# Chunk attention and two expert layers: the value products of one tile and the scores of the next put into one sequence

## The chip, the cores and the metric

The kernel runs on one core of a Trainium2 chip. The metric is the device time of one execution in microseconds (us). Six engines are named: PE (TensorE, matmuls), PEld (its weight loads), DVE (VectorE), ACT (ScalarE), POOL (GpSimd) and SP (SyncE, which issues DMAs).

## The reference

Three stages follow one another; the output of each is the input of the next.

```python
# 1. attention inside chunks of 64: q, k, v of (8 batches, 8 heads, 576, 64)
scores = (q_c @ k_c^T) / sqrt(64);  scores -= max(scores)
attn = exp(scores);  attn = attn / (sum(attn) + 1e-9);  x = attn @ v_c
x -> (4608 tokens, 512)
# 2. first layer: d_model 512, d_ff 1536
g = x @ w_gate;  x2 = (g * sigmoid(g) * (x @ w_val)) @ w_out
# 3. second layer: d_ff 2048
h = x2 @ w_in;  out = (h - tanh(h)) @ w_out2
```

## The kernel before

**Layers.** Tokens are worked in 9 blocks of 512. The hidden columns of a layer are worked in pairs of 128-wide tiles. The first layer makes two sweeps over the blocks with three pairs each (sweep 0 and sweep 1), the second layer one sweep with eight pairs. One pair of one block is a *unit* of 22 slots. Numbers are split into a high and a low part and multiplied in three passes, so a product of two blocks is a group of matmuls "x3" or "x6". The in-projections use a scheme of seven block products (inputs named B11, B21, T2, T1, T3, B22, T4, tiles `xb_*`); their outputs are `Xg, Yg` (gate) and `Xv, Yv` (value), in banks m0 and m1. DVE and ACT make the two parts of each `xb` tile: a cast (the high part, steps `x0.hB11` and so on) and a subtraction (the low part, `x0.lB11`). The out-projections are `acc`, in banks o0 to o3. In the page L1239 is the out-projection and L660 an in-projection.

**Attention.** It runs inside sweep 0, one block ahead: during the three units of block t-1 the four tiles of block t are worked, each a pair of heads (tile numbers 8 to 35, function `heads`) or a group of tokens (4 to 7, `tokens`; 0 to 3 run at the start and are called early). Steps of a tile, with their names in the tables: q and k are loaded (`lq`, SP) and turned (`tq`, `tk`, DVE), v is loaded (`lv`, POOL's queue). PE makes 16 products of 64x64 for each half of the tile, `sc` (step `s`, L887, 32 matmuls in all). DVE takes the maximum and subtracts it (`c0`, `c1`: tiles `mx`, `scratch`), ACT takes the exponential (`e`), DVE the sums (`n`, tile `sm`) and the division (`m`, L302), PE turns the result (`p`, `ppt`, L823), ACT copies it, PE makes the products with v, `po` (step `o`, L898, 32 matmuls), and ACT copies these to the block's x, `xra`. Both `sc` and `po` lie in PSUM banks a0 and a1, a pair of tiles each, one after the other; `ppt` too lies in a0.

**Order.** Nothing is scheduled on the chip: a table `AT` gives each step a slot relative to the start of its set (`START`, for attention tiles a0 to a3 in each block), `ON` names the engine (A for ACT, V for DVE), and `tick` issues, after each piece of PE work, all steps whose slot has come. Every engine then works its instructions in that order. A PE piece is one group of six in-projection matmuls or three out-projection matmuls.

Of the kernel before, what the change touches and what calls it, by code (L numbers as in the profile page):

```python
# [10 lines left out]
F32 = mybir.dt.float32  # L11
# [18 lines left out]
    "ah.ld": -6.5, "ah.mag": 9.5, "ah.cl": 11.5, "ah.sh": 11.5, "ah.sg": 12.5, "ah.tl": 13,  # L30
# [12 lines left out]
    "g1.l0": 19.5, "g1.h1": 22, "g1.l1": 23, "a.lq": -19.5, "a.lv": 4, "a.tq": -8.5, "a.tk": -4,  # L43
    "a.s": 0, "a.c0": 1.5, "a.c1": 2.5, "a.e": 3, "a.n": 7, "a.m": 9, "a.p": 12.5, "a.o": 14.5,
    "ge.silu0": 14.5, "ge.silu1": 12.5, "ge.m1": 21, "ge.m0": 20.5, "ge.h0": 23, "ge.l0": 24.5,
    "ge.h1": 24, "ge.l1": 32, "dr.ld": -19.5, "dr.mag": 9, "dr.cl": 11, "dr.sh": 11.5,
    "dr.sg": 13, "dr.tl": 13, "dr.h": 16.5, "dr.l": 17.5, "dc.ld0": -14, "dc.mag0": 0,
# [195 lines left out]
def chunk_attention_moe_moe(  # L243
# [14 lines left out]
    nc = tc.nc  # L258
# [5 lines left out]
    HP = H // 2  # L264
    C = 64
# [1212 lines left out]
```

## Time and profile before

| | |
|---|---|
| median of 3 runs | 1757.7 us (1754.9 to 1758.71) |
| profiled execution | 1756.21 us, its span 1754.4 us |
| mean granted clock of TensorE | 0.994 of full speed |
| PE busy | 1712.4 us (98%) |
| DVE busy | 1381.9 us (79%) |
| ACT busy | 1135.8 us (65%) |

The span falls into four parts here: the start (0 to 100 us, attention of the first block, weights are split), the rest of sweep 0 (100 to 500 us, with the attention of the later blocks in it), the passage to sweep 1 (500 to 600 us), and the rest. A row of the windows view gives, for a stretch "from:to", its length, then the busy time and the number of instructions of PE, PEld, DVE, ACT and POOL, then TensorE's granted clock, the share of the DMA engines and GB/s. A row of the timeline gives the start of a group of like instructions, the time from its first start to its last end, engine, line, operation and tile; in brackets the idle time before it and what ended it. Neighbouring PE groups overlap in that view, because matmuls are pipelined: what a group costs is read from start to start. A row of the waits view gives what waited, for what, the time in total, how often, and the longest.

### The profile page before, as it was taken

What the parts mean: (1) busy time and instruction counts of PE and PEld (TensorE: products, weight loads), DVE (VectorE), ACT (ScalarE), POOL (GpSimd) and SP (SyncE); (2) the same over time, 40 slices, a digit from 0 to 9 for tenths busy, and PEclk for the clock granted to TensorE, in tenths of its full rate; (3) what the DMA queues carried; (4) which work ended last, traced back from release to release, by engine and by line L of the source; (5) the groups of instructions that cost most, each with busy time, mean ns of one, the idle gap of its engine ahead of it and who ended that gap; (6) DMA issues with size and microseconds to landing.
All of it is one profiled execution on the core that took longest, in us unless ns stands there. A gap on an engine that the chain in (4) does not pass through costs nothing.

```text
span 1754.4 us, 33741 instructions
## 1 busy us (share of the span) xinstructions
PE 1712.4 (98%) x12880; PEld 1531.7 (87%) x12880; DVE 1381.9 (79%) x2613; ACT 1135.8 (65%) x2209; POOL 136.5 (8%) x238
## 2 busy tenths in 40 slices
PE   5999999999999999999999999999999999999999
PEld 4778888888898999999999898899999898998997
DVE  6998778887878987787875678787877878787876
ACT  4765565566555655545554578787777777777776
POOL 2133333322100000000000000000000000000000
PEclk8999999999999999999999999999999999999999
DMA  9554554555423555555545744343434343434333
GB/s 244 143 109 115 142 134 123 128 145 138 131 101 120 193 186 169 180 186 186 169 167 191 260 174 145 107 145 97 151 102 144 105 148 97 149 104 144 99 130 109
DMA packets 238482, 254.94 MB, mean 145 GB/s; under 512 B 150000, under 2 KB 175472, under 8 KB 236016
## 3 DMA queue, kind: packets, MB, share of 16 engines
q1 hardware_dynamic: 230896, 243.33, 45.4%
q0 software_dynamic: 7424, 9.45, 2.1%
q8 instruction: 101, 1.65, 0.4%
q14 instruction: 61, 0.50, 0.1%
HBM read 187.17 MB, written 65.54 MB: 144 GB/s over the span
## 4 chain that ended last, share of the span: by engine, by line
PE 83%; DVE 8%; SPq 4%; DMA 3%; ACT 1%; issue 1%; DVEq 0%; ACTq 0%
PE acc L1239 36%; PE Xi L660 12%; PE Yi L660 9%; PE Xg L660 6%; PE Xv L660 6%; PE Yv L660 5%; PE Yg L660 5%; SPq L849 3%; DMA raw_wv<-in_moe_w_val_dram 1%; SPq L947 1%; DMA kr<-in_k_dram 1%; DVE scratch L299 1%; PE po L898 1%; PE sc L887 1%; PE ppt L823 1%
## 5 line engine op out<-in xcount | busy, mean ns | idle before, releaser
L1239 PE MATMUL acc<-wp,h 128*128 128x512 f32 x1728 | 479.9, 394 | 0.0
L1239 PE MATMUL acc<-h,wo 128*128 128x512 f32 x1296 | 364.1, 397 | 0.0
L1239 PEld LDWEIGHTS acc<-wp,h 128*128 128x128 f32 x1728 | 290.9, 188 | 33.4 <-DVE h L299 0.3
L1239 PEld LDWEIGHTS acc<-h,wo 128*128 128x128 f32 x1296 | 220.4, 189 | 28.6
L338 ACT CAST h<-gs 128x512 fp32r<-128x512 f32 x144 | 89.5, 621 | 86.0 <-DVE gs L1150 84.5
L864 POOL DMA_DIRECT2D vr<-in_v_dram x200 | 116.2, 599 | 283.9 <-PE po L898 259.9
L660 PEld LDWEIGHTS Xg<-xb_T,wg 128*128 128x128 f32 x864 | 122.2, 188 | 13.0
L660 PE MATMUL Xg<-xb_T,wg 128*128 128x256 f32 x864 | 125.9, 281 | 0.0
L296 DVE TENSOR_TENSOR gs<-Yi,s 128x256 f32<-128x256 f32 x144 | 60.8, 422 | 64.9 <-PE Yi L660 59.5
L1073 ACT ACTIVATE gs<-gs 128x512 f32<-128x512 f32 x96 | 60.8, 633 | 58.0 <-DVE gs L296 57.8
L299 DVE TENSOR_TENSOR vr<-gs,vr 128x512 f32<-128x512 f32 x72 | 49.9, 692 | 54.6 <-ACT vr L1126 54.6
L299 DVE TENSOR_TENSOR h<-gs,h 128x512 fp32r<-128x512 f32 x144 | 92.7, 684 | 0.2 <-ACT h L338 0.2
L338 ACT CAST h<-vs 128x512 fp32r<-128x512 f32 x107 | 66.3, 622 | 37.1 <-PE acc L1239 25.2
L299 DVE TENSOR_TENSOR h<-vs,h 128x512 fp32r<-128x512 f32 x108 | 73.6, 682 | 20.3 <-ACT h L338 19.5
L660 PE MATMUL Yv<-xb_B,wv 128*128 128x256 f32 x576 | 85.4, 283 | 2.0 <-ACT s L338 1.9
L660 PE MATMUL Xv<-xb_T,wv 128*128 128x256 f32 x576 | 86.2, 285 | 0.8 <-ACT sqr L338 0.8
L660 PE MATMUL Yg<-xb_B,wg 128*128 128x256 f32 x576 | 84.2, 281 | 0.0
L660 PEld LDWEIGHTS Yg<-xb_B,wg 128*128 128x128 f32 x576 | 78.8, 189 | 5.1
L660 PEld LDWEIGHTS Yv<-xb_B,wv 128*128 128x128 f32 x576 | 75.4, 188 | 6.1 <-ACT s L338 4.6
L660 PEld LDWEIGHTS Xv<-xb_T,wv 128*128 128x128 f32 x576 | 75.1, 189 | 1.4 <-ACT sqr L338 1.0
L338 ACT COPY s<-Xi 128x256 f32<-128x256 f32 x144 | 53.5, 372 | 34.9 <-PE Xi L660 30.9
L302 DVE TENSOR_TENSOR vs<-vs,gs 128x512 f32<-128x512 f32 x96 | 65.8, 686 | 8.1 <-ACT gs L1073 5.3
(310 smaller groups left out, 3732.7 us busy)
## 6 DMA issues: line engine op xcount, KB each, us to landing
wp<-split_wp SPq DMA_DIRECT2D x144, 512.0 KB, 3.5
split_wi<-wi SPq DMA_DIRECT2D x24, 512.0 KB, 3.4
xd<-xra SPq DMA_DIRECT2D x36, 256.0 KB, 3.1
x2p<-ob SPq DMA_DIRECT2D x36, 256.0 KB, 2.6
xr_xd<-xd SPq DMA_DIRECT2D x9, 1024.0 KB, 4.8
ob<-x2p SPq DMA_DIRECT2D x36, 256.0 KB, 4.2
x2d<-ob SPq DMA_DIRECT2D x36, 256.0 KB, 2.4
xr_x2d<-x2d SPq DMA_DIRECT2D x9, 1024.0 KB, 6.0
```

Of the source, the lines that this page charges most:

```text
L296: eng.tensor_tensor(out=out_, in0=a, in1=b, op=ALU.add)
L299: eng.tensor_tensor(out=out_, in0=a, in1=b, op=ALU.subtract)
L302: eng.tensor_tensor(out=out_, in0=a, in1=b, op=ALU.mult)
L338: eng.copy(out_, in_)
L660: nc.tensor.matmul(bank, w[:, wl, kk * 128:(kk + 1) * 128], x[xn][:, xl, kk, :], start=start and n == 0, stop=n == 5, skip_group_check=not ...
L823: nc.tensor.transpose(pt[:, m, :], z["p"][:, m].rearrange("p e j -> p (e j)"), ident)
L849: nc.sync.dma_start(out=r[p:p + 32, 2 * n:2 * (n + m)], in_=src[b, 2 * j + e, s:s + m * C, d * 32:d * 32 + 32] .rearrange("(n p) d -> p n ...
L864: nc.gpsimd.dma_start(out=vr[p:p + C, n + skip:n + m:2], in_=chunks[:, skip:m:2],)
L887: nc.tensor.matmul(sc[e ^ c][c * C:(c + 1) * C, m, :], z["qT"][h, cut], z["kT"][h, cut], start=True, stop=True,)
L898: nc.tensor.matmul(po[c][h, m, :], z["vr"][f, 2 * m + c, :], z["pT"][f, m, c * C:(c + 1) * C], start=True, stop=True,)
L1073: return lambda: nc.scalar.activation(out=gs[i], in_=gs[i], func=AF.Silu)
L1239: nc.tensor.matmul(u["acc"][d], l, r, start=p0 and i == 0 and n == 0, stop=p1 and i == 1 and n == 2,)
```

## The change

Two functions made the `sc` and the `po` of a tile by themselves. Now a function `burst(g, n)` makes the `po` of tile g and the `sc` of tile n = g+1 in one sequence, four of the one and four of the other in turn, into a pair of tiles in banks a0 and a1 that hold both: `po` in the first half of a bank, `sc` in the second. It stands at the step `o` of tile g. Step `s` is gone for tiles 5 to 35; tile 4's scores come alone (`burst(None, 4)`) and tile 35's products with v alone. The early tiles 0 to 3 stay as they were. So there were 64 sequences of 32 matmuls outside the early tiles, and there are now 31 of 64 matmuls and two of 32.

```diff
+    def burst(g, n):
+        bank = [
+            ps.tile([128, 2, 4, C], F32, tag=f"a{c}", name=f"po{g}_sc{n}_{c}") for c in range(2)
+        ]
+        half = [slice(0, C), slice(C, 2 * C)]
+        if g is not None:
+            z = att[g]
+            z["po"] = [bank[c][:, 0] for c in range(2)]
+        if n is not None:
+            y = att[n]
+            y["sc"] = [bank[e][:, 1] for e in range(2)]
+            done.add((("a", n), "s"))
+        for m in range(4):
+            if g is not None:
+                for c in range(2):
+                    for e in range(2):
+                        f = half[e ^ c]
+                        nc.tensor.matmul(
+                            z["po"][c][half[e], m, :], z["v_"](f, m, c), z["pT"][f, m, half[c]],
+                            start=True, stop=True,
+                        )
+            if n is not None:
+                for c in range(2):
+                    for e in range(2):
+                        nc.tensor.matmul(
+                            y["sc"][e ^ c][half[c], m, :],
+                            y["q_"](half[e], m, c), y["k_"](half[e], m, c),
+                            start=True, stop=True,
+                        )
...
         def output(eng):
-            po = [ps.tile([128, 4, C], F32, tag=f"a{c}", name=f"po{g}_{c}") for c in range(2)]
...
+            burst(g, g + 1 if g + 1 < NG else None)
+            po = z["po"]
...
-        step("s", scores, ["tq", "tk"])
```

Beside it the tables for sweep 0 have other numbers: 267 of the 614 slots that both tables name. Of attention's steps `c0`, `c1` and `e` keep their slots after a tile's start; the rest are later or earlier:

```diff
-    "g1.l0": 19.5, "g1.h1": 22, "g1.l1": 23, "a.lq": -19.5, "a.lv": 4, "a.tq": -8.5, "a.tk": -4,
-    "a.s": 0, "a.c0": 1.5, "a.c1": 2.5, "a.e": 3, "a.n": 7, "a.m": 9, "a.p": 12.5, "a.o": 14.5,
+    "g0.l1": 33.5, "g1.silu0": 16, "g1.silu1": 21, "g1.m1": 22, "g1.m0": 16.5, "g1.h0": 18.5,
+    "g1.l0": 23, "g1.h1": 23, "g1.l1": 27, "a.lq": -23.5, "a.lv": 8, "a.tq": -3, "a.tk": -3,
+    "a.c0": 1.5, "a.c1": 2.5, "a.e": 3, "a.n": 8, "a.m": 9.5, "a.p": 13.5, "a.o": 16.5,
...
-    "units": 60, "a0": -12, "a1": 4, "a2": 20, "a3": 38, "ah0": 140, "ah0 every": 22,
+    "units": 60, "a0": -12, "a1": 4.5, "a2": 21, "a3": 38, "ah0": 140, "ah0 every": 22,
```

Fifteen entries of `ON` differ. Five casts of the next block (`x0.hB11`, `x0.hB21`, `x0.hT2`, `x0.hT3`, `x0.hB22`) go from DVE to ACT, two of sweep 1 (`x1.hT3`, `x1.hT4`) from ACT to DVE, and eight single steps change sides.

**PE, around the products with v of tile 24.** The rows of before, where a block of six or three matmuls is one row:

```order
L823 MATMUL ppt24_4607<-ident_81,scratch0_175 128x128 x4
L660 MATMUL Xg0_5_0_4631<-xb14_B11_4497,wg0_0_592 128x256 x6
L660 MATMUL Yg0_5_0_4632<-xb14_B21_4499,wg0_0_592 128x256 x6
L898 MATMUL po24_0_4654<-scratch0_175,vr24_4532 64x64 x2
...
L898 MATMUL po24_1_4655<-scratch0_175,vr24_4532 64x64 x2
L1239 MATMUL acc0_4_0_0_4357<-h0_4_1_1_4381,wo1_1_1252 128x512 x3
L660 MATMUL Xg0_5_0_4631<-xb14_T2_4515,wg0_1_1656 128x256 x6
L887 MATMUL sc0_25_4688<-kT25_4605,qT25_4570 64x64
L887 MATMUL sc1_25_4689<-kT25_4605,qT25_4570 64x64 x2
```

And the same place after the change:

```order
L822 MATMUL ppt24_4590<-ident_81,scratch0_175 128x128 x4
L659 MATMUL Yg0_5_0_4581<-xb14_B21_4472,wg0_0_590 128x256 x6
L1260 MATMUL acc0_4_0_0_4300<-h0_4_1_1_4392,wo1_1_1255 128x512 x3
L659 MATMUL Xg0_5_0_4580<-xb14_T2_4475,wg0_1_1660 128x256 x6
L850 MATMUL po24_sc25_0_4624<-scratch0_175,vr24_4524 64x64 x2
L850 MATMUL po24_sc25_1_4625<-scratch0_175,vr24_4524 64x64 x2
L857 MATMUL po24_sc25_0_4624<-kT25_4598,qT25_4596 64x64
L857 MATMUL po24_sc25_1_4625<-kT25_4598,qT25_4596 64x64 x2
L857 MATMUL po24_sc25_0_4624<-kT25_4598,qT25_4596 64x64
L850 MATMUL po24_sc25_0_4624<-scratch0_175,vr24_4524 64x64 x2
```

The scores of tile 25 stood two pieces behind the products with v; now both are one run of rows that write the same two tiles. Three pieces instead of two stand between `ppt24` and the products.

**DVE, from the maximum of tile 24 to its division, in the third unit of a block.** Before; the names in brackets are the engines that the row waits for:

```order
L796 TENSOR_REDUCE mx24_0_4493<-sc0_24_4465 128x4 [waits PE_49]
...
L340 CAST xb14_B11_4497<-xra5_3825 128x512 [waits PE_49]
L340 CAST xb14_B21_4499<-xra5_3825 128x512 [waits PE_49]
...
L340 CAST xb14_T2_4515<-scratch1_2011 128x512 [waits PE_49]
...
L873 STREAM_TRANSPOSE qT25_4570<-qr25_4401 128x512 [waits DMAHW4_49,DMAHW5_49,DMAHW3_49,DMAHW6_49,DMAHW2_49,DMAHW7_49,DMAHW1_49,DMAHW0_49]
L296 TENSOR_TENSOR vs0_4_2_0_4509<-Yv0_4_2_4484,s0_4_2_4485 128x256 [waits PE_49]
L340 CAST xb14_T3_4580<-xra5_3825 128x512 [waits DVE_49]
L302 TENSOR_TENSOR scratch0_175<-scratch0_175,sm24_4565 128x512
```

After:

```order
L795 TENSOR_REDUCE mx24_0_4455<-po23_sc24_0_4407 128x4 [waits Activation_49]
...
L298 TENSOR_TENSOR xb14_B21_4472<-xra5_3819,xb14_B21_4472 128x512 [waits Activation_49]
...
L301 TENSOR_TENSOR scratch0_175<-scratch0_175,sm24_4533 128x512 [waits DVE_49]
L298 TENSOR_TENSOR xb14_T1_4508<-xra5_3819,xb14_T1_4508 128x512 [waits Activation_49]
L298 TENSOR_TENSOR xb14_T3_4510<-xra5_3819,xb14_T3_4510 128x512 [waits Activation_49]
L301 TENSOR_TENSOR vs0_4_2_0_4465<-vs0_4_2_0_4465,gs0_4_2_0_4298 128x512
L907 STREAM_TRANSPOSE qT25_4596<-qr25_4328 128x512 [waits DMAHW4_49,DMAHW5_49,DMAHW3_49,DMAHW6_49,DMAHW2_49,DMAHW7_49,DMAHW1_49,DMAHW0_49]
L907 STREAM_TRANSPOSE kT25_4598<-kr25_4337 128x512 [waits DMAHW4_49,DMAHW5_49,DMAHW3_49,DMAHW6_49,DMAHW2_49,DMAHW7_49,DMAHW1_49,DMAHW0_49]
```

The first maximum waited for PE; now it waits for ACT, whose two copies of `po23` (out of the same banks) come first. Between it and the division 21 rows stood, now 15: the four casts are on ACT, and the turn of q of tile 25 (and one addition to `h`) stand outside this stretch.

## Rows read from the trace of the kernel before

**Rows 1.** Page, busy time of each engine and share of the span.

```profile
PE 1712.4 (98%) x12880; PEld 1531.7 (87%) x12880; DVE 1381.9 (79%) x2613; ACT 1135.8 (65%) x2209; POOL 136.5 (8%) x238
```

**Rows 2.** Windows view, four parts of the span: length, PE, PEld, DVE, ACT, POOL.

```profile
0.00:100.00 100.00, 77.01 (x812) 59.96 (x813) 80.71 (x178) 59.94 (x106) 24.82 (x46) 0.90 0.79 185
100.00:500.00 400.00, 390.43 (x4007) 339.87 (x4006) 323.71 (x685) 240.16 (x453) 111.67 (x192) 1.00 0.52 128
500.00:600.00 100.00, 95.64 (x652) 87.41 (x652) 83.51 (x173) 58.55 (x128) 0.00 (x0) 1.00 0.44 155
600.00:1754.40 1154.40, 1149.36 (x7415) 1044.43 (x7413) 893.98 (x1581) 777.14 (x1524) 0.00 (x0) 1.00 0.44 147
```

**Rows 3.** Waits view of PE, 100 to 500 us: total, times, longest.

```profile
PE ppt L823 <- DVE scratch L302: 6.5, 8, 1.1
PE Yv L660 <- ACT s L338: 1.3, 5, 0.4
PE po L898 <- ACT scratch L338: 0.9, 4, 0.2
```

**Rows 4.** Timeline of PE around one sequence of scores: start, duration, group.

```profile
308.32 0.88 PE L660 MATMUL Xv<-xb_T,wv 128*128 128x256 f32 x6
309.12 0.69 PE L887 MATMUL sc<-kT,qT 64*64 64x64 f32 x32
309.75 0.96 PE L1239 MATMUL acc<-h,wo 128*128 128x512 f32 x3
310.54 0.52 PE L660 MATMUL Yv<-xb_B,wv 128*128 128x256 f32 x3
```

**Rows 5.** The same view where no 64x64 sequence stands between.

```profile
314.08 0.87 PE L660 MATMUL Yg<-xb_B,wg 128*128 128x256 f32 x6
314.79 0.86 PE L1239 MATMUL acc<-h,wo 128*128 128x512 f32 x3
315.49 0.87 PE L660 MATMUL Xg<-xb_T,wg 128*128 128x256 f32 x6
```

**Rows 6.** One line's matmuls, L898: shortest, median and longest in ns, first and last start.

```profile
L898 PE MATMUL po<-scratch,vr x896: 218/218/268, 110.9 to 494.2; 64*64 64x64 f32 x180
```

**Rows 7.** Timeline of PE in the start, two 64x64 sequences on end.

```profile
31.57 0.96 PE L998 MATMUL sc<-kT,qT 64*64 64x64 f32 x32
32.35 1.11 PE L1025 MATMUL po<-pp,vr 64*64 64x64 f32 x32
33.39 0.66 PE L823 MATMUL ppt<-ident,pp 128*128 128x128 f32 x4
```

**Rows 8.** Windows view, a third unit of a block and a stretch in that start.

```profile
330.40:349.80 19.40, 18.18 (x177) 15.85 (x175) 17.49 (x38) 11.58 (x22) 4.51 (x8) 1.00 0.45 116
...
32.30:33.40 1.10, 1.10 (x49) 1.03 (x41) 1.10 (x3) 0.00 (x0) 0.00 (x0) 1.00 1.19 278
```

**Rows 9.** Timeline of DVE, from the maximum of tile 24 to its division.

```profile
323.60 0.42 DVE L796 TENSOR_REDUCE mx<-sc 128x4 f32<-128x256 f32 x1 [0.70 <-PE sc L887]
...
325.00 0.78 DVE L340 CAST xb_B<-xra 128x512 fp32r<-128x512 f32 x2
...
327.42 0.42 DVE L340 CAST xb_T<-scratch 128x512 fp32r<-128x512 f32 x1
...
332.08 0.70 DVE L873 STREAM_TRANSPOSE qT<-qr 128x512 f32<-128x512 f32 x1
...
333.34 0.68 DVE L302 TENSOR_TENSOR scratch<-scratch,sm 128x512 f32<-128x512 f32 x1
```

**Rows 10.** Timeline of PE, the transposition that waits for that division.

```profile
334.17 0.63 PE L823 MATMUL ppt<-ident,scratch 128*128 128x128 f32 x4 [1.07 <-DVE scratch L302]
```

**Rows 11.** Timeline of ACT behind the products with v of tile 24.

```profile
337.44 0.65 ACT L338 COPY xra<-po 128x256 f32<-128x256 f32 x2 [0.95 <-PE po L898]
...
341.50 1.28 ACT L801 ACT_TABLE_LOAD   x1
```

**Rows 12.** Waits view of PE, 500 to 600 us, the two largest.

```profile
PE Yg L660 <- DVE gs L296: 1.7, 1, 1.7
PE Xg L660 <- DVE vs L296: 1.1, 1, 1.1
```

More of the change, by code (lines that the diff above doesn't have):

```diff
@@ L29 @@
 AT = {
-    "ah.ld": -6.5, "ah.mag": 9.5, "ah.cl": 11.5, "ah.sh": 11.5, "ah.sg": 12.5, "ah.tl": 13,
[12 rows of a table removed]
-    "g1.l0": 19.5, "g1.h1": 22, "g1.l1": 23, "a.lq": -19.5, "a.lv": 4, "a.tq": -8.5, "a.tk": -4,
-    "a.s": 0, "a.c0": 1.5, "a.c1": 2.5, "a.e": 3, "a.n": 7, "a.m": 9, "a.p": 12.5, "a.o": 14.5,
-    "ge.silu0": 14.5, "ge.silu1": 12.5, "ge.m1": 21, "ge.m0": 20.5, "ge.h0": 23, "ge.l0": 24.5,
-    "ge.h1": 24, "ge.l1": 32, "dr.ld": -19.5, "dr.mag": 9, "dr.cl": 11, "dr.sh": 11.5,
-    "dr.sg": 13, "dr.tl": 13, "dr.h": 16.5, "dr.l": 17.5, "dc.ld0": -14, "dc.mag0": 0,
[3 rows of a table removed]
+    "ah.ld": -13, "ah.mag": 10.5, "ah.cl": 12, "ah.sh": 13, "ah.sg": 13.5, "ah.tl": 28.5,
[12 rows of a table added]
+    "g1.l0": 23, "g1.h1": 23, "g1.l1": 27, "a.lq": -23.5, "a.lv": 8, "a.tq": -3, "a.tk": -3,
+    "a.c0": 1.5, "a.c1": 2.5, "a.e": 3, "a.n": 8, "a.m": 9.5, "a.p": 13.5, "a.o": 16.5,
+    "ge.silu0": 20, "ge.silu1": 20, "ge.m1": 24, "ge.m0": 21.5, "ge.h0": 23.5, "ge.l0": 24,
+    "ge.h1": 29, "ge.l1": 34.5, "dr.ld": -22.5, "dr.mag": 9, "dr.cl": 11, "dr.sh": 11.5,
+    "dr.sg": 13, "dr.tl": 13, "dr.h": 16.5, "dr.l": 17.5, "dc.ld0": -13.5, "dc.mag0": 0.5,
[3 rows of a table added]
     "dc.l1": 24, "dc.h2": 22, "dc.l2": 26, "fc2.ld0": -2, "fc2.ld1": 11, "fc2.ld2": -4,
@@ L827, in turn_p @@
         return f
+    att = {}
+    def burst(g, n):
[7 more added lines that the diff above has]
+        if n is not None:
+            assert (("a", n), "tq") in done and (("a", n), "tk") in done
+            y = att[n]
[18 more added lines that the diff above has]
+                        )
     def heads(g, start):
@@ L876, in turn, with chunk @@
             return f
-        def scores():
-            sc = z["sc"] = [
-                ps.tile([128, 4, C], F32, tag=f"a{e}", name=f"sc{e}_{g}") for e in range(2)
-            ]
-            for m in range(4):
-                for c in range(2):
-                    cut = slice((2 * m + c) * C, (2 * m + c + 1) * C)
-                    for e in range(2):
-                        h = slice(e * C, (e + 1) * C)
-                        nc.tensor.matmul(
-                            sc[e ^ c][c * C:(c + 1) * C, m, :], z["qT"][h, cut], z["kT"][h, cut],
-                            start=True, stop=True,
-                        )
-        def output(eng):
-            po = [ps.tile([128, 4, C], F32, tag=f"a{c}", name=f"po{g}_{c}") for c in range(2)]
-            for m in range(4):
-                for c in range(2):
-                    for e in range(2):
-                        h, f = slice(e * C, (e + 1) * C), slice((e ^ c) * C, ((e ^ c) + 1) * C)
-                        nc.tensor.matmul(
-                            po[c][h, m, :], z["vr"][f, 2 * m + c, :],
-                            z["pT"][f, m, c * C:(c + 1) * C],
-                            start=True, stop=True,
-                        )
+        def chunk(nm):
+            return lambda h, m, c: z[nm][h, (2 * m + c) * C:(2 * m + c + 1) * C]
+        att[g] = z
+        z["q_"], z["k_"] = chunk("qT"), chunk("kT")
+        z["v_"] = lambda f, m, c: z["vr"][f, 2 * m + c, :]
+        def output(eng):
+            burst(g, g + 1 if g + 1 < NG else None)
+            po = z["po"]
             if j == 0:
@@ L934, in tokens @@
         else:
-            banks = dict(q="a0", k="a1", s=("a0", "a1"), p="a0", o="a1")
+            banks = dict(q="a0", k="a1", p="a0")
+            att[g] = z
+            z["q_"] = lambda h, m, c: z["qT"][h, m, c * C:(c + 1) * C]
+            z["k_"] = lambda h, m, c: z["kT"][h, m, c * C:(c + 1) * C]
+            z["v_"] = lambda f, m, c: z["vr"][f, c, m, :]
         def load_qk():
@@ L998, in scores @@
                         nc.tensor.matmul(
-                            sc[e if early else e ^ c][i, hp, :], z["qT"][h, hp, i], z["kT"][h, hp, i],
+                            sc[e][i, hp, :], z["qT"][h, hp, i], z["kT"][h, hp, i],
                             start=True, stop=True,
@@ L1013, in output @@
                 po = ps.tile([128, HP, 128], F32, tag=banks["o"], name=f"po{g}")
-                whole, po = po, [po[:, :, :C], po[:, :, C:]]
-            else:
-                po = [
-                    ps.tile([128, HP, C], F32, tag=banks["s"][c], name=f"po{g}_{c}")
-                    for c in range(2)
-                ]
-            for hp in range(HP):
-                for c in range(2):
-                    for e in range(2):
-                        h, i = slice(e * C, (e + 1) * C), slice(c * C, (c + 1) * C)
-                        f = h if early or c == 0 else slice((1 - e) * C, (2 - e) * C)
-                        nc.tensor.matmul(
-                            po[c][h, hp, :], z["vr"][f, c, hp, :], z["pT"][f, hp, i],
-                            start=True, stop=True,
-                        )
+                for hp in range(HP):
+                    for c in range(2):
+                        for e in range(2):
+                            h, i = slice(e * C, (e + 1) * C), slice(c * C, (c + 1) * C)
+                            nc.tensor.matmul(
+                                po[h, hp, i], z["vr"][h, c, hp, :], z["pT"][h, hp, i],
+                                start=True, stop=True,
+                            )
+            else:
+                burst(g, g + 1)
+                po = z["po"]
             if j == 0:
@@ L1033, in output @@
             if early:
-                copy(eng, xp, whole)
+                copy(eng, xp, po)
             else:
@@ L1046, in tokens @@
         step("tk", turn(1), ["lq"])
-        step("s", scores, ["tq", "tk"])
+        if early:
+            step("s", scores, ["tq", "tk"])
+        elif g == SUB:
+            step("s", lambda: burst(None, g), ["tq", "tk"])
         softmax(step, g, scratch_of, [] if early else before)
```

228 rows, old and new, of tables (AT, ON, START) are left out of this document.

## The prediction

> **What bounds the kernel now.** I read the page's engine line first: PE is busy 98% of the span, no other engine over 79% [rows 1]. So time can be won only by taking work from PE or by closing PE's holes, and the next view is where those holes are. The windows view [rows 2], length minus PE busy: 100 − 77.0 = 23.0 us in the start, 400 − 390.4 = 9.6 us in the rest of sweep 0, 100 − 95.6 = 4.4 us in the passage to sweep 1, and 1154.4 − 1149.4 = 5.0 us in the 1154 us after it, next to nothing. From 100 us on the granted clock is 1.00, so there is nothing to win there. The third view is what PE waited for in the second part [rows 3]: the transposition of the attention weights (`ppt`) for DVE's division, 6.5 us in 8 waits, the longest 1.1; the value in-projection for ACT's copies, 1.3; the products with v for ACT's copy of the turned weights, 0.9.
>
> The fourth view shows what the busy time hides: the cost of a 64x64 sequence, read from start to start. From the Xv group at 308.32 to the Yv group at 310.54, with a group of scores and three out-projection matmuls between, it is 2.22 us [rows 4]. The same two groups without scores take 315.49 − 314.08 = 1.41 us [rows 5]. So one sequence of 32 records costs PE 0.81 us. Inside the sequence the matmuls start within 0.69 − 0.22 = 0.47 us of one another (0.69 is first start to last end [rows 4], 218 ns is one record [rows 6]). The other 0.81 − 0.47 = 0.34 us is entering and leaving, when PE goes from full-width matmuls to quarter-size ones and back.
>
> **The change, part by part.** All sums are made against the profiled execution's 1756.21 us (span 1754.4 and 1.8 around it). The runs' median, 1757.7, stands 1.5 us above it, and I add that at the end.
>
> *Merging.* 64 sequences become 33, so 31 times one entering and leaving goes: 31 × 0.34 = 10.5 us, all on PE and in a stretch where PE is busy 97.6%. No row shows products with v and scores in turn. Bounds: against the gain, every alternation could cost a step of its own. A merged sequence has 7 alternations, and one step of four records takes 0.47 / 8 = 0.06 us, so 0.42 us lost against 0.34 saved: 31 × 0.08 = 2.5 us slower. On the other side nothing more than the 0.34 can go, −10.5. The nearest row is in the start, where `po` follows `sc` without anything between: the last score starts at 31.57 + 0.96 − 0.22 = 32.31 and the first product with v at 32.35 [rows 7]. No hole of 0.34 is there. The rows stand at a changing clock (it is 1.00 from 32.30 [rows 8]), but a hole would only be longer at a lower one. The order also shows that each group of four still goes once over the four quarters of the array, as before. I take −10.5.
>
> *The wait for the division.* In the third unit of each block DVE is busy 17.5 of 19.4 us [rows 8]. There `ppt` of tile 24 stands still 1.07 us [rows 10], waiting for a division that ends at 334.02, 10.4 us after DVE took up the maximum at 323.60 [rows 9]. After the change four casts (0.78 for two, 0.42, and one more like it) and the turn of q (0.70) have left the rows between these two points, 2.3 us [rows 9]. PE has 13 pieces instead of 12 between the scores and `ppt`, 0.7 us more room (314.08 to 314.79 is one [rows 5]). Against it stands a new wait: DVE's first maximum now comes behind ACT's two copies of `po`, 0.65 us [rows 11]. Behind that maximum DVE's whole queue stands: the sums for the next block's `xb`, the `h` of the out-projection, the exponential's input; PE waits for all of them in the end. 2.3 + 0.7 − 0.65 = 2.35 us against the stall of 1.07: a reserve of 1.3 us per block. Some of it goes, because DVE's subtractions for `xb14` now wait for casts that stand on ACT. So the `ppt` waits shrink from 6.5 to 1.2, −5.3. Later than before could be the turn of k of tile 25, which now has to be ready for the merged sequence: five DVE rows behind the division, some 0.6 each, against `ppt` (0.4 from its start to the next group) and three pieces of 0.7. That is 3.0 against 2.5, covered by the reserve.
>
> *The smaller waits of sweep 0.* `po` for ACT's copy, 0.9: three pieces instead of two stand before the products, room 0.7 more against single waits of at most 0.2, so it goes. `Yv` for ACT, 1.3, I halve, −0.7: ACT is given casts there, but it is busy 240 of 400 us [rows 2]. For new waits I add +1.5 (eight blocks, 0.2 each). Sum of this and the division: −5.3 − 0.9 − 0.7 + 1.5 = −5.4; bounds 0 (all of it moves elsewhere) and −9.6 (all idle time of the stretch).
>
> *The passage to sweep 1.* PE waits 1.7 and 1.1 us for DVE, once each [rows 12]. There the order of DVE changes: weight splits for sweep 1 stand earlier, the two waited-for sums (`gs`, `vs`) stand ahead of rows of the last split instead of behind, and casts go to ACT. I take −2.5; bounds 0 and −4.4, all the idle time [rows 2].
>
> *The start.* Tiles 0 to 3 keep their own sequences, and DVE's chain there (80.7 of 100 us busy [rows 2]) stands nearly as before: 0, bounds −1.5 and +1.5, a small part of the 23.0.
>
> *At nothing.* The q and k loads stand earlier on SP, some before the stores of x; where such a load has to wait for the turn of the tile before (its buffer is single), stores queue behind it. What is stored is read a sweep later, and the q and k are needed some 20 slots (17 us) after the load. If that cover were gone, the turn would be late and the merged sequence with it, which is inside the +1.5 and the bound of 0. The v loads stand 8 slots ahead of the products instead of 10, some 7 us; POOL is busy 112 of 400 [rows 2]. Five casts per block go from DVE to ACT and two per block of sweep 1 back: ACT is at 60% in the one, DVE at 77% in the other [rows 2], and PE has no holes in the latter to show that anything is near.
>
> Sum: −10.5 − 5.4 − 2.5 = −18.4, so 1756.2 − 18.4 = 1737.8, and with the 1.5 to the median 1739.3.
>
> **A rule that speaks against it.** The order shows the first maximum waiting for ACT where it waited for PE, although the two read different halves of a bank. The Trainium skill ("PSUM — Partial Sum Buffer", section "PSUM bank collisions raise a hardware error") says why: two engines may not be on the same quadrant of a bank at once, reads beside reads included, even in other columns. No run here shows such a collision. Without the rule the maximum could begin with the copies, the reserve would be 1.95 and not 1.3, and the third rival below would have no mechanism; its chance would be the forecast's.
>
> **Rivals.**
> *Merging pays, the waits only move* (0.22). DVE stays near its bound in the third unit, and whatever goes from the division turns up at the turn of k, at ACT's casts or at `h`. For it: the stretch was already at 97.6%, and the new order makes two steps (`pT` and both turns) due at one point. Against it: 2.3 us of DVE work really leave the tight place. Time: 1756.2 − 10.5 + 1.5 = 1747.2, median 1748.7.
> *The alternation does not stream* (0.08): the change does not give what merging is for. Sequences cost as much as before, or up to the +2.5. For it: no row shows the alternation. Against it: rows 7. The waits still go, −7.9: 1748.3 to 1750.8, and with the 1.5 about 1751.
> *Copies before the maximum make it slower* (0.04). In every tile the softmax starts 0.65 later, and in one of four the copies stand behind a table load of 1.28 [rows 11]. If all of that reached PE: 31 × 0.65 + 8 × 1.28 = 30.4 against 10.5, 1776.1, median 1777.6. It decides once more than 10.5 / 31 = 0.34 us per tile reaches PE. Against it: DVE is idle 400 − 323.7 = 76 us in the stretch [rows 2], some 2.7 us for each of 28 tiles.
> *The forecast* 0.60. 0.06 is left for what I don't see (the start, half of it slower).
>
> **How the numbers follow.** The forecast's own range is 1732 to 1744 (all idle time closed: 1756.2 − 10.5 − 9.6 − 4.4 + 1.5 = 1733, and the start's −1.5; up: 4 or 5 us of waits that stay). With the two rivals up to 1751 the range is 1731 to 1751. A measurement of this kernel can tell about 0.2%, 3.5 us, from no change: same is 1754.2 to 1761.2. Faster by more: forecast, the first rival, most of the second and a little of the rest: 0.91. Same 0.05, slower 0.04.
>
> **What would show it.** In the profile after, between 100 and 500 us: (1) a merged sequence of 64 records with some 1.3 us from start to start beyond its neighbours, where two cost 1.62; (2) PE busy in sweep 0 shorter by some 10 us, and the end of sweep 0 some 16 us earlier; (3) `ppt` waiting for the division under 2 us in all; (4) the 500 to 600 waits on DVE's `gs` and `vs` gone or below 1 us. I am wrong on merging if a merged sequence costs 1.6; on the waits if PE's idle time in the stretch stays at 9 us or more; on all of it if the maximum's wait for ACT shows up as PE waiting for DVE in every tile.

## The result and the profile after

The changed kernel takes 1726.6 us (median of 4 runs, 1724.7 to 1728.2) against 1758.2 us for the kernel before (4 runs). The ratio is 0.9823, interval [0.9803, 0.9842]: faster by 31.6 us in the medians, 18.4 forecast, and outside the range of 1731 to 1751. The two profiled executions differ by less, 1756.21 and 1728.19 us, 28.0, since the one of before lies below its median and the one of after is the slowest of its four.

The same four windows of the changed kernel [rows 2]; columns: stretch, length, busy us of PE, PEld, DVE, ACT, POOL, granted clock, DMA share, GB/s:

```profile
0.00:100.00 100.00, 76.83 (x812) 60.11 (x813) 82.79 (x181) 57.29 (x101) 24.81 (x46) 0.90 0.77 184
100.00:500.00 400.00, 398.63 (x4168) 360.38 (x4168) 328.66 (x691) 266.44 (x508) 111.26 (x192) 1.00 0.54 134
500.00:600.00 100.00, 99.44 (x684) 91.52 (x683) 88.75 (x181) 63.05 (x139) 0.00 (x0) 1.00 0.50 171
600.00:1726.10 1126.10, 1120.94 (x7222) 1019.17 (x7220) 877.40 (x1551) 752.07 (x1475) 0.00 (x0) 1.00 0.44 147
```

PE's holes went from 9.6 to 1.4 us in sweep 0 and from 4.4 to 0.6 in the passage; the start is as it was. PE's waits between 100 and 500 us [rows 3], all that the view lists:

```profile
PE ppt L822 <- DVE scratch L301: 1.4, 1, 1.4
```

And in the passage [rows 12]:

```profile
PE Xg L659 <- DVE vs L295: 0.3, 1, 0.3
PE Xv L659 <- DVE gs L295: 0.2, 1, 0.2
```

A merged sequence in PE's timeline, to be read beside [rows 4]:

```profile
309.45 0.88 PE L659 MATMUL Xg<-xb_T,wg 128*128 128x256 f32 x6
310.26 0.34 PE L850 MATMUL po_sc<-scratch,vr 64*64 64x64 f32 x8
310.43 0.30 PE L857 MATMUL po_sc<-kT,qT 64*64 64x64 f32 x8
...
311.13 0.30 PE L857 MATMUL po_sc<-kT,qT 64*64 64x64 f32 x8
311.36 0.98 PE L659 MATMUL Xv<-xb_B,wv 128*128 128x256 f32 x6
312.18 0.52 PE L659 MATMUL Yv<-xb_B,wv 128*128 128x256 f32 x3
```

From 309.45 to 312.18 two groups of six and 64 records take 2.73 us; two groups of six alone are some 1.43 (0.71 to 0.72 each). So the sequence costs some 1.29 us where two cost 2 × 0.81 = 1.62. (Each of the 32 products in it leaves two records, so a group of four products is a row "x8".) The seven alternations show no step of their own: but for the first, the groups of eight start 0.11 to 0.12 us apart.

**Where the time went, from start to start.** For every pair of neighbouring matmuls I took the distance of their starts less the usual one for the two shapes (0.118 us behind a 256-column matmul, 0.23 behind a 512-column one, and so on), and called the rest a hole; what stands around a 64x64 sequence was put to the sequence, its waits with it. From the first to the 541st matmul of the out-projection (82 to 511 us before, 82 to 487 after: sweep 0 behind the start) and from there to 600 us (the passage) this gives, in us:

| | stretch | sequences (number) | holes, sweep 0 | holes, passage |
|---|---|---|---|---|
| before | 429.0 | 48.1 (57) | 19.0 | 6.7 |
| after | 405.3 | 36.9 (29) | 6.5 | 2.2 |
| difference | −23.8 | −11.2 | −12.6 | −4.5 |

−11.2 − 12.6 − 4.5 = −28.3, all of the difference of the two spans (1754.4 and 1726.1). The levels of the holes hang on the usual distances (1 ns more in each takes some 2 us off the 19.0 and off the 6.5); the differences do not, because the stretch holds the same matmuls in both kernels.

### The profile page after: what moved, and what is told of

Read it like the earlier page. It is cut to its first block, busy times and chain, and to the rows that moved or that the text cites. A ratio compares the mean times of both kernels' runs of the same rounds, so it can differ in the third digit from the quotient of the medians.

```text
span 1726.1 us, 33806 instructions
## 1 busy us (share of the span) xinstructions
PE 1695.8 (98%) x12880; PEld 1531.2 (89%) x12880; DVE 1377.6 (80%) x2601; ACT 1138.8 (66%) x2221; POOL 136.1 (8%) x238
## 4 chain that ended last, share of the span: by engine, by line
PE 94%; DVE 2%; DMA 1%; ACT 1%; SPq 1%; issue 0%; DVEq 0%; ACTq 0%
PE acc L1260 39%; PE Xi L659 12%; PE Yi L659 9%; PE Xv L659 8%; PE Xg L659 8%; PE Yg L659 6%; PE Yv L659 6%; PE po_sc L850 1%; PE ppt L822 1%; PE Xg L714 1%; PE Yv L714 1%; PE po_sc L857 1%; PE Yg L714 1%; SPq L969 1%; DMA qr<-in_q_dram 1%; PE Xv L714 1%
## 5 line engine op out<-in xcount | busy, mean ns | idle before, releaser
L898 POOL DMA_DIRECT2D vr<-in_v_dram x200 | 115.8, 594 | 263.2 <-PE po_sc L857 249.9
```

Source lines behind the costliest of these rows:

```text
L898: nc.gpsimd.dma_start(out=vr[p:p + C, n + skip:n + m:2], in_=chunks[:, skip:m:2],)
```

## The experiments

Each kernel is the changed one but for its edit, unless it says otherwise. Medians are set against the kernel before as measured beside them (1756.4 to 1757.0; beside the changed kernel it stood at 1758.2, so distances to 1726.6 hold to some 2 us). The last three columns are the sums explained above, in us.

| run | median us | ratio to before | sequences | holes, sweep 0 | passage |
|---|---|---|---|---|---|
| merge alone | 1762.6 | 1.0031 [1.0021, 1.0042] | 47.7 | 24.8 | 6.7 |
| scores one piece ahead | 1745.9 | 0.9935 [0.9923, 0.9948] | 56.0 | 6.0 | 2.3 |
| in two blocks | 1727.0 | 0.9828 [0.9814, 0.9841] | 36.9 | 6.8 | 1.9 |
| inputs' slots back | 1736.7 | 0.9886 [0.9870, 0.9901] | 42.4 | 10.2 | 4.8 |
| merge, attention's slots | 1759.3 | 1.0016 [1.0007, 1.0026] | 50.2 | 21.8 | 7.8 |
| full-width matmul inside | 1741.5 | 0.9916 [0.9901, 0.9930] | 51.9 | 5.1 | 2.5 |
| gates' slots back | 1732.3 | 0.9871 [0.9853, 0.9888] | 37.1 | 11.2 | 2.6 |
| weights' slots back | 1748.3 | 0.9955 [0.9940, 0.9969] | 44.0 | 16.7 | 6.1 |
| ahead set back | 1741.6 | 0.9915 [0.9900, 0.9930] | 44.4 | 12.1 | 2.3 |
| unmerged, other slots new | 1747.0 | 0.9948 [0.9933, 0.9962] | 50.6 | 11.5 | 2.4 |
| one turn later | 1723.5 | 0.9815 [0.9801, 0.9830] | 36.8 | 4.9 | 2.4 |
| attention's slots back | 1752.8 | 0.9975 [0.9964, 0.9985] | 49.6 | 17.2 | 2.3 |

**1. Merge alone.** The tables of before under the new code; `+    "b7.o": 125.3,` is the one other number.

> The merged sequences with the slots, engines and starts of the kernel before; only tile 7's products with v stand 3.8 slots later (its step o at 125.3), since the next tile's q and k have to be turned first. Theory (two separate gains): merging saves 31 x 0.36 = 11 us and the tables the rest by closing holes of PE. Then this one takes 1758 - 11 = 1747 us, and read from start to start PE's holes in sweep 0 stay at some 19 us. Rival (merging itself closes the holes, because banks a0 and a1 change hands half as often): 1727 to 1733 us, holes under 8.

Both theories missed: it is slower than the kernel before. PE's waits, 100 to 500 us:

```profile
PE ppt L820 <- DVE scratch L299: 8.2, 8, 1.2
PE po_sc L855 <- DVE kT L905: 7.8, 7, 1.5
```

The median sequence costs 1.30 us, so merging saves its 0.34 us a time here too. But the sequences' sum hardly falls (47.7 against 48.1), since waits ahead of them take the saving back, above all one for `kT` that the kernel before did not have (7.8 us by the view); and the holes grow (24.8 against 19.0). In the old order the turn of k of the next tile is not due until two pieces after the products with v; in one sequence it is due with them. The same wait as DVE has it, in the third unit of a block: the division ends at 339.58, and three more rows stand before the turn of k.

```profile
338.90 0.68 DVE L299 TENSOR_TENSOR scratch<-scratch,sm 128x512 f32<-128x512 f32 x1
339.50 0.69 DVE L296 TENSOR_TENSOR xb_T<-xra,xb_T 128x512 fp32r<-128x512 f32 x1
340.10 0.42 DVE L337 CAST xb_B<-xra 128x512 fp32r<-128x512 f32 x1
340.43 0.69 DVE L299 TENSOR_TENSOR vs<-vs,gs 128x512 f32<-128x512 f32 x1
341.04 0.70 DVE L905 STREAM_TRANSPOSE kT<-kr 128x512 f32<-128x512 f32 x1
```

**2. Scores one piece ahead.** The merging undone under the new tables, by calls of `burst` with a part each:

```diff
+        if g + 1 < NG:
+            issue(start + AT[f"{step.name}.o"] - 1, lambda: burst(g, g + 1, 0))
...
-            burst(g, g + 1 if g + 1 < NG else None)
+            burst(g, g + 1 if g + 1 < NG else None, 1)
```

> The changed kernel, new tables, but the scores of tile g+1 run one PE piece ahead of the products with v of tile g, as two sequences of 32 into the same shared banks. Theory (two separate gains): 31 enterings come back, 1727 + 11 = 1738 us, and the holes in sweep 0 stay at some 6.5 us. Rival (merging closes the holes): 1750 us or more, holes over 15. Third possibility (merging is worth nothing, the tables all): 1727.

1745.9 lies between the two. Holes stay at 6.0 us as the theory said, but the sequences cost 56.0 us and not some 47, since the earlier scores now wait for the turn of k (6.6 us in 17 waits). So this undoes more than the merging, and its 19 us are no price of it.

**3. In two blocks.**

```diff
-        for m in range(4):
-            if g is not None:
+        for m in range(8):
+            if g is not None and m < 4:
...
+            m -= 4
+            if n is not None and m >= 0:
```

> The changed kernel, but within a merged sequence all 16 products with v stand first and then all 16 scores, with one alternation and not seven. Theory (the gain is one entering less, the turn-taking costs and gives nothing): 1727 within 3 us, a sequence takes 1.28 us as before. Rival (an alternation costs a step of 0.06 us): 31 x 6 x 0.06 = 11 us less, 1716. Rival (the turn-taking overlaps the two, and that is the gain): 3 us or more slower.

1727.0, as the theory had it: turn-taking costs and gives nothing. In the timeline 32 products with v and 32 scores follow one another:

```profile
308.73 0.69 PE L850 MATMUL po_sc<-scratch,vr 64*64 64x64 f32 x32
309.25 0.65 PE L858 MATMUL po_sc<-kT,qT 64*64 64x64 f32 x32
309.82 0.98 PE L659 MATMUL Xv<-xb_B,wv 128*128 128x256 f32 x6
```

**4. A full-width matmul inside.**

```diff
         for m in range(4):
+            if m == 2 and g is not None and n is not None:
+                nc.tensor.matmul(
+                    y["sc"][0][:, 3, :], ident, z["pT"][:, 0, :C], start=True, stop=True,
+                )
```

> The changed kernel with one full-width matmul (the identity by 64 columns, into a place that the next products overwrite) in the middle of each of the 31 merged sequences. Theory (what merging saves is one entering and leaving, 0.36 us): each sequence grows by 0.36 and the matmul's own 0.06 to 0.11, 31 x 0.42 to 0.47 = 13 to 15 us, 1740 to 1742. Rival (the saving comes from fewer waits, not from the switch itself): the matmul alone, 2 to 3.5 us, 1729 to 1730.

1741.5, 14.9 us more than the changed kernel and where the theory put it. The median sequence grows from 1.287 to 1.810 us. The hole ahead of the added matmul and the one behind it can be read:

```profile
318.78 0.30 PE L861 MATMUL po_sc<-kT,qT 64*64 64x64 f32 x8
319.01 0.43 PE L847 MATMUL po_sc<-scratch,ident 128*128 128x64 f32 x2
319.38 0.34 PE L854 MATMUL po_sc<-scratch,vr 64*64 64x64 f32 x8
```

Eight records otherwise take 0.12 us to the next group; here 0.23, and from the added matmul to the next products 0.37. That is the switch with the matmul's own time, 0.48 us here, in a kernel with few other holes (5.1 us); 31 of them cost 14.9 us.

**5 to 10. The tables in four parts.** Of the slots that differ in both tables (259; the 267 of the section on the change count the eight steps `s` that are gone too), 28 belong to the next block's inputs (x0, x1), 38 to the gates, 64 to attention and 129 to weights and passage. Five runs put one part back to its old numbers (of the last part also the ahead set alone), and one has the new numbers of attention alone. As an example the ahead set, whole:

```diff
-    "ah.ld": -13, "ah.mag": 10.5, "ah.cl": 12, "ah.sh": 13, "ah.sg": 13.5, "ah.tl": 28.5,
-    "ah.st": 28.5,
+    "ah.ld": -6.5, "ah.mag": 9.5, "ah.cl": 11.5, "ah.sh": 11.5, "ah.sg": 12.5, "ah.tl": 13,
+    "ah.st": 25.5,
```

Inputs back (engines too):

> The changed kernel, with slots and engines of the next block's inputs alone (all steps x0 and x1, 28 slots and 7 engines) as before: five casts per block are DVE's again. Theory (the wait for the division went because these casts left DVE's third unit): the holes ahead of ppt come back, 1.2 us in each of 6 or 7 blocks, 1727 + 7 to 8 = 1735 us. Rival (the new slots of attention alone give the room): 1727 within 3 us, ppt's holes stay under 2 us.

1736.7: the size is the theory's, its place is not. The holes ahead of `ppt` stayed closed (1.6 us, as after); what came back is the wait for the turn of k, 4.1 us in 5 waits, holes at Yv and Xv, and 2.6 us in the passage. So these slots and engines serve the turn of k; whether by the five casts that left DVE or by the new slots, the run can't tell.

Attention's slots alone new:

> Merged sequences with the new slots of attention alone (64 slots, 4 engines, the starts a1 and a2); all other steps stand as in the kernel before. Theory (the merged sequence needs the turn of k and the copy of the weights at one point, and only later slots let both be ready): the waits for kT shrink from 7.8 us in sweep 0 to under 4 and those of ppt from 8.2 to under 3, 1758 - 11 - 8 + 4 = 1743 us; the holes of the passage stay at 6.7 us. Rival (the casts are what keeps DVE late): kT and ppt waits stay over 10 us together, 1755 us or more.

The rival's time and more: 1759.3, but not its waits. Those of `ppt` did shrink, 8.2 to 3.0 us, those for `kT` only to 4.5, together 7.5; a third appeared, for ACT (6.0 us in 5 waits, below).

Gates back:

> The changed kernel with the slots and engines of the gate's steps (silu, product, splits of the hidden block: 38 slots, 3 engines) as before. Theory (the in-projection's holes, Yv and Xv behind ACT's copies and DVE's sums, closed because the silu with its table load went out of their way): the holes behind Yv and ahead of it come back, some 5 us, 1732 us. Rival (they closed because the casts or attention's steps moved): 1727 within 3 us.

1732.3, the theory's number; the waits for ACT's copies come back, though at Yg and not at Yv (`PE Yg L657 <- ACT s L335: 1.7, 5, 0.3`; start to start, five holes of 0.50 us).

Weights and passage back:

> The changed kernel with the slots of the weights and of the passage to sweep 1 (129 slots, one engine, all starts but a1 and a2) as before. Theory (the passage's holes closed by the new order of the weight splits): sweep 0 as in the changed kernel, the passage's holes back to 6.7 us, 1727 + 4.5 = 1731 us. Rival (they closed because sweep 0's work no longer runs into it): 1727 within 3 us.

The passage is as expected (6.1 us), but 1748.3 is 17 us above the theory's time: sweep 0 has 44.0 us of sequences and 16.7 us of holes, 36.9 and 6.5 in the changed kernel. I had taken these slots for work of the passage alone.

The ahead set alone back:

> The changed kernel with the seven slots of the set that converts sweep 1's weights ahead (steps ah: one load, one ACT step, four DVE steps in a row, one store, once per unit of sweep 0) as before. Theory (the 21.7 us that the weights' slots gave lie in this set, since it alone of them runs through all of sweep 0): 1727 + 10 or more, 1737 to 1748 us, with PE's sequences waiting for ACT and the turns in every block. Rival (the slots of the first block's weights and of the passage gave them): 1727 within 4 us.

1741.6, as the theory had it: 15 us for seven slots. PE's waits, 100 to 500 us:

```profile
PE po_sc L848 <- ACT scratch L335: 6.9, 4, 2.6
PE ppt L820 <- DVE scratch L299: 2.4, 7, 1.4
```

The new one is the wait for ACT's copy of the turned weights. ACT at one of these places, and SP's queue before it:

```profile
198.62 0.37 ACT L335 COPY s<-Yg 128x256 f32<-128x256 f32 x1 [0.35 <-PE Yg L657]
204.08 0.66 ACT L364 ACTIVATE cvt_wg<-raw_wg 128x512 f32<-128x512 f32 x1 [5.08 <-DMA raw_wg<-in_moe_w_gate_dram]
204.64 0.57 ACT L335 COPY scratch<-ppt 128x512 f32<-128x512 f32 x1
```

```profile
188.80 4.77 SPq L881 DMA_DIRECT2D qr<-in_q_dram  x8
193.66 5.16 SPq L881 DMA_DIRECT2D kr<-in_k_dram  x8
198.93 0.39 SPq L1231 DMA_DIRECT2D x2p<-ob  x1
199.36 0.43 SPq L351 DMA_DIRECT2D raw_wg<-in_moe_w_gate_dram  x1
```

The q and k loads, now issued earlier, hold SP for ten microseconds; the weight load behind them leaves at 199.36, ACT stands 5.1 us for it, and the copy of `ppt` for which PE waits (2.0 us there) stands behind ACT. In the changed kernel the load stands ahead of the q and k loads:

```profile
184.90 0.43 SPq L353 DMA_DIRECT2D raw_wg<-in_moe_w_gate_dram  x1
188.00 4.64 SPq L883 DMA_DIRECT2D qr<-in_q_dram  x8
```

So attention's earlier loads need the ahead set's still earlier one. The third wait of the run with attention's slots alone has the same picture: there SP is held by q and k loads from 195.12 to 204.63, `raw_wg` leaves at 205.17, and the sequence at 212.10 has waited 2.54 us for ACT's copy.

Attention's slots back:

> The changed kernel, merged, with attention's own slots as before (64 slots, 4 engines, a1 and a2; tile 7's step o at 125.3, as in the merge-only run). Theory (the merged sequence needs the copy of the weights and the turn of k at one point; the old slots put it 2 slots too early): PE waits for kT or ppt 8 us or more in sweep 0, 1735 to 1740 us. Rival (the relief on DVE by the other slots is enough): 1727 within 3 us.

1752.8, worse than either: PE waits 7.2 us for `kT` and 6.4 at `ppt`. With those slots old, merging loses (next run). That the old slots put the point just two slots too early is not shown.

**11. Unmerged, other slots new.** The kernel before with the new numbers of inputs, gates, weights and passage.

> The kernel before, unmerged, attention's own steps where they stood, with the new slots, engines and starts of everything else (next block's inputs, gates, weights, passage). Theory (the order of that work closes holes of PE by itself, merging or not): holes of sweep 0 from 19 to under 9 us, passage from 6.7 to 2.5 us, 1757 - 14 = 1743 us or less. Rival (these slots only fit the merged sequences): 1754 us or more.

1747.0, between the theory (1743 or less) and the rival, nearer the theory: holes 19.0 to 11.5 us and the passage to 2.4. The holes missed the theory's 9 us, and the sequences cost 2.5 us more: the weight loads of `sc` wait 3.4 us for ACT's copies of `po`, 0.7 before. So this order gains 9.6 us without merging. Against it the run before shows what merging adds while attention's slots are old: 5.8 us slower.

**12. One turn later.** `-    "h11.tk": 167.25,` `+    "h11.tk": 171.2,`. The one large hole left in the changed kernel: DVE stands 1.68 us before the turn of k of tile 11, and the maxima of tile 10, and so its `ppt`, stand behind that turn.

```profile
129.93 0.71 DVE L907 STREAM_TRANSPOSE kT<-kr 128x512 f32<-128x512 f32 x1 [1.68 <-DMA x2p<-ob]
130.56 0.39 DVE L795 TENSOR_REDUCE mx<-po_sc 128x4 f32<-128x256 f32 x1
```

```profile
135.64 0.63 PE L822 MATMUL ppt<-ident,scratch 128*128 128x128 f32 x4 [1.37 <-DVE scratch L301]
```

The view puts DVE's wait down to a store (`x2p`), and the expectation below has the load queued behind it; that is not shown. SP's queue has the loads of k leave from 123.10 to 127.60 and that store behind them, and the kernel before, where the load and this turn have the same slots, stands at the same place with the load itself named:

```profile
123.10 4.50 SPq L883 DMA_DIRECT2D kr<-in_k_dram  x8
127.70 0.41 SPq L1233 DMA_DIRECT2D x2p<-ob  x1
```

```profile
130.20 0.71 DVE L873 STREAM_TRANSPOSE kT<-kr 128x512 f32<-128x512 f32 x1 [1.45 <-DMA kr<-in_k_dram]
```

(The first two rows are of the changed kernel, the third of the kernel before; there PE's `ppt` waited 0.30.)

> The changed kernel with one slot of the table changed: the turn of k of tile 11 3.95 slots later (171.2), behind the two maxima of tile 10 on DVE. In the changed kernel this turn stands idle 1.68 us for its load, whose DMA is queued behind a store, and the maxima and ppt of tile 10 queue behind it. Theory: the one hole ahead of ppt that is left (1.5 us) goes, 1725.2 us, at the edge of what the rounds tell; in the trace ppt of tile 10 no longer waits. Rival: the turn is late for the sequence then, and PE waits there instead, 1727.

The hole went (6.5 to 4.9 us in the stretch). PE is then busy throughout:

```profile
100.00:500.00 400.00, 400.00 (x4184) 362.15 (x4184) 329.60 (x695) 266.92 (x511) 111.09 (x192) 1.00 0.53 135
```

1723.5 us is the lowest median here, 0.9815 to the kernel before; its interval holds the changed kernel's 0.9823, so only the 1.5 us of the trace are shown.

## Why the prediction was wrong

*Merging: right.* −10.5 was forecast for 31 merges. The stretch holds 28 of them: 28 × (2 × 0.82 − 1.29) = 9.9 us by the median sequences, and the other 1.3 of its −11.2 are waits ahead of sequences that went. The full-width run prices 31 switches at 14.9 us with an added matmul each, and the two-block run says that the alternation costs nothing. The second rival (it does not stream) is out. Its bound was read wrong, without effect: a group of four products is eight records and 0.12 us, not four and 0.06.

*The waits: the step that failed.* I took PE's holes as "length minus PE busy", 9.6 us and 4.4, and made them the ceiling of what the tables could give (−5.4 taken, −9.6 the bound). Start to start the stretches of the table held 19.0 and 6.7 us, of which 12.6 and 4.5 went. Two things were wrong: of the ceiling I took too little, since even by the idle time 8.2 and 3.8 us went, 12.0 where −5.4 − 2.5 = −7.9 was forecast; and the ceiling was too low. By distances all the waits together gave 12.6 + 4.5 + 1.3 = 18.4 us, beside merging's 9.9. It is the ceiling that put the time below the range, whose lower end already had all idle time closed. The idle time understates a hole, because the record of a 256-column matmul lasts 0.28 us and the next usually starts after 0.12: a wait up to the difference leaves no idle time, a longer one is shown short. A place of before that I passed over:

```profile
327.89 0.86 PE L1239 MATMUL acc<-h,wo 128*128 128x512 f32 x3
329.00 0.97 PE L660 MATMUL Yv<-xb_B,wv 128*128 128x256 f32 x6 [0.24 <-ACT s L338]
```

The starts lie 1.11 us apart where they otherwise lie 0.70 [rows 5], a hole of 0.41; the view says 0.24. `ppt` in [rows 10] waits 1.07 by the view and 1.23 from start to start. The weight loads would have told it. Their waits of before, 100 to 500 us, the six largest lines but one:

```profile
PEld ppt L823 <- issue: 9.0, 7, 1.5
PEld po L898 <- ACT scratch L338: 4.2, 8, 0.7
PEld Yv L660 <- ACT s L338: 3.5, 5, 0.8
PEld Yv L660 <- DVE vs L296: 3.1, 6, 0.6
...
PEld Xv L660 <- DVE vs L296: 1.3, 5, 0.3
```

and after, the first three:

```profile
PEld po_sc L850 <- ACT vs L337: 2.2, 6, 0.4
PEld ppt L822 <- issue: 1.8, 1, 1.8
PEld po_sc L850 <- DVE scratch L339: 0.4, 1, 0.4
```

In the first list Yv waits 3.1 us for DVE's sums, a cause that PE's own waits [rows 3] do not name at all. The loads' busy share of the stretch says the same: 85% before (339.9 of 400 [rows 2]), 90% after. The Trainium skill ("Perfetto Trace Analysis", section "Identifying the Most-Contended Engine") warns that the matmul's busy share is no good measure of how close PE is to its peak, and asks for the weight loads' share and the share of peak arithmetic. The trace agrees on the loads: PE went from 98% to 100% of the stretch, they from 85% to 90%. The page's reason is that pipelined matmuls look smaller in the trace; here their records look larger, 0.28 us where the next starts after 0.12.

*New waits.* I added +1.5 as eight small ones. The view shows one, 1.4 us at tile 10, where DVE stood for a load before the change too: the size agrees by luck. No `ppt` waits in the third units, so the reserve that I worked out there held.

*What I cost at nothing.* Inside the change no wait shows a cost of the earlier q and k loads (the load behind the 1.4 us of tile 10 has its old slot). But I said that stores alone queue behind them; the weight loads do too, and without the ahead set's earlier load that costs 15 us. Moving the casts costs nothing, as I said; but with all the inputs' slots and engines back (+10 us) it is the turn of k that comes late, not the division.

*The first rival* (merging pays, waits only move) describes the merge-alone kernel, though worse: 1762.6. *The third* did not occur: DVE's maxima do wait for ACT's copies,

```profile
DVE mx L795 <- ACT xra L337: 11.0, 9, 1.6
```

but with the new tables no `ppt` waits but the one.

What stays open is how the gain splits. Putting back inputs, gates, weights or attention costs 10, 6, 22 and 26 us, 64 together and twice the gain, so the parts depend on one another and no sum over them means anything. Nor was the merging undone in a way that moved nothing else.

## What to carry to other kernels

Before bounding what a new order can give a busy PE, measure its holes from start to start, or read the weight loads' waits: here "98% busy" hid nearly half of the holes (14.0 us by idle time, 25.7 by distances). A merged sequence makes two chains due at one point; its own gain (0.35 us a time here) is kept only if the later chain, its engine and its loads are moved ahead with it, so price the merge in the old order too. When a load is moved ahead on an in-order queue, look at every load behind it, and at who stands behind its consumer.

## What the runs showed of the hardware

A switch from full-width matmuls to 64x64 ones and back costs 0.34 to 0.35 us (0.81 − 0.47 in [rows 4], 2 × 0.82 − 1.29 in the medians), beside 0.47 us for the 32 records themselves. Products with v and scores in turn run at the pace of either alone (64 records in 0.94 us from first to last start, 32 in 0.48). The sixteen loads of q and k of one tile held SP's queue for 9.9 us (4.77 and 5.16, run with the ahead set back).
